# Nine weight pieces stored from another engine's queue, and one two-piece load split, in a recurrent-memory attention kernel

## The chip, the cores and the metric

The kernel runs on one core of a Trainium2 chip. The metric is the time of the whole program on the device in microseconds (us). The version before the change took a median of 2320.83 us in three runs (2319.13 to 2324.82).

## The reference, cut to what matters

Two independent branches see the same input `x` (2048 tokens of width 1024) and are mixed by a gate. Branch A is attention with 32 heads of 128 over segments of 32 tokens; eight memory rows, taken from the output of one segment, are put ahead of the next segment. So the 64 segments depend on each other. Branch B is a GeGLU feed-forward network of width 3584.

```python
for s in range(n_seg):                       # 64 segments, one after another
    h = concat([mem, x[:, 32*s:32*s+32]])    # 8 memory rows + 32 tokens
    q, k, v = h @ Wq, h @ Wk, h @ Wv         # each weight: 1024 x 32 x 128
    p = softmax(mask(q @ k.T * scale))
    o = (p @ v) @ Wo                         # Wo: 32 x 128 x 1024
    mem, out[s] = o[:, :8], o[:, 8:]
b = (gelu(x @ w_gate) * (x @ w_up)) @ w_down
return g * a + (1 - g) * b                   # g = sigmoid(sum(x * gate_w))
```

## The kernel before

**Segments.** One step of the kernel is one segment. A step's TensorE work has eight projections: `k`, `q`, `v` and `o`, each for two halves of 16 heads. `r` = 0 is the half that comes first in the step and `r` = 1 the other; which heads those are (`u`) alternates from step to step (`at_step`, L325). Each projection is cut into eight pieces of weights, 128 partitions x 2048 bf16 (512 KB). `walk` (L328) writes out the order of the pieces in a step: `HEAD` holds the first four pieces of `k`, two of `q`, the *last four pieces of the step before's second* `o`, and the rest of `k`, `q`, `v`; `BODY` holds the second halves of `k` and `q`, the first `o`, the second `v`, and the first four pieces of the second `o`. Everything else of a step (evacuations of PSUM, transposes, scores, softmax, attention, stores) is hung on a place of this walk: `on("o", 1, 0, f)` in `plan` (L903) emits `f` ahead of piece 0 of the second `o`. An engine executes its instructions in the order of emission.

**Fill.** Besides the step's own work TensorE projects 8 rows of each segment some steps ahead (`fill`, L844). The results are evacuated by ScalarE (`fill_evac`) into staging tiles, of which `0S` and `1S` lie over the tiles `hT` and `oRc`.

**Weights.** SBUF doesn't hold all pieces. A slot that two pieces share (`PAIRS`, L311: two of k, two of q, five of v, five of o) is loaded twice a step. When a piece has been used, `spent` (L442) emits the load of the slot's next one, on SP's queue. Pieces of neighbouring slots are loaded by one DMA: `GROUPS` (L372) tells how many. `spent` holds a used piece back until all of its group are used, and then `load_group` (L422, DMA on L429 from scratch or L433 from the inputs) loads them together, here Wo 0 and 1 (1 MB) and Wo 4, 5 and 6 (1.5 MB). Wo pieces that aren't all in scratch yet are loaded one by one (L385, L387). The first `o` uses pieces in pairs (0,4), (1,5), (2,6), (3,7) on L798 and frees 0 after the first pair, 1, 4, 5 after the second and 6 after the third. The second `o` (L815) uses 2, 3, 0, 1 in `BODY`, and 7, 4, 5, 6 in the next step's `HEAD`.

**Stores.** In the first steps each shared piece is written once from its slot to a scratch buffer of the group's layout (`keep`, L389, DMA on L391), so that later loads read long rows. Wo pieces are stored in steps 1 to 10 at `("k", 0, 4)`. The pieces of v, k and q (`STORE`, L901: v0 to v4, k0, k1, q0, q1, each for both halves) are stored in steps 3 to 20 at `("o", 1, 0)`, one a step: v in steps 3 to 12, k in 13 to 16, q in 17 to 20. All stores go through SP's queue and share one semaphore lane, so each waits for the landing of the store before. A load into a slot waits until the slot's store has landed.

**Behind the stores on SP.** At `("o", 1, 0)` SP also issues the load of `qkr` for the next step (L542) and the store of `oRc` to `o_scr` (L991). ScalarE's evacuation into `0S` or `1S` (L663) has to wait for that last store to land, TensorE transposes the tile on L680, and the next loads of k, q and v follow on SP.

The rest of the program (the output projection of eight rows of each segment, and the feed-forward network from L1074) isn't touched.

Of the kernel before, what the change touches and what calls it, by code (L numbers as in the profile page):

```python
# [30 lines left out]
class _Prog:  # L31
# [47 lines left out]
    def op(self, eng, fn, rd=(), wr=(), lane=None, after=()):  # L79
        o = _Op(eng, fn)  # L80
        if lane is not None:
            ln = self.lanes.get(lane)
            if ln is None:
                ln = self.lanes[lane] = [self.new_sem(f"{self.name}_{lane}"), 0, None]
            if ln[2] is not None:
                o.deps.append(ln[2])
            ln[1] += 16
            o.sem, o.val, o.inc, o.need = ln[0], ln[1], 16, True
            ln[2] = o
        for r in rd:  # L90
            self._touch(o, r, False, lane is not None)
        for r in wr:
            self._touch(o, r, True, lane is not None)
        o.deps.extend(after)
        if eng == "pool" and lane is None:
            if self.pool is not None:
                o.deps.append(self.pool)
            self.pool = o
        for d in o.deps:
            d.need = True  # L100
        o.idx = len(self.ops)
        self.ops.append(o)
        return o
# [107 lines left out]
def bass_gated_mix__memory_aug_recurrent_mem_tr__geglu_ffn__prompt_kernel(  # L211
# [16 lines left out]
    S, D = xf.shape  # L228
# [17 lines left out]
    with ExitStack() as es:  # L246
# [78 lines left out]
        def at_step(s, m, r, n):  # L325
            return (m, r ^ (s % 2), seq(m, r)[n])

        walk = []  # L328
        for s_ in range(NSEG):
            for m, r, lo, hi in HEAD + BODY:  # L330
                e = s_ - ((m, r, lo) == ("o", 1, 4))
# [20 lines left out]
        for _, e, m, r, n in walk:  # L352
            k = at_step(e, m, r, n)
# [3 lines left out]
        op = P.op  # L357
# [11 lines left out]
        def dst(t, k):  # L369
            return t[:, :].rearrange("p (h f) -> p h f", h=4) if k[0] == "o" else t[:, :]  # L370

        GROUPS = {("k", 0): 2, ("q", 0): 2, ("v", 0): 3, ("v", 3): 2, ("o", 0): 2, ("o", 4): 3}  # L372
        lead = {(m, i + x): (m, i) for (m, i), n in GROUPS.items() for x in range(n)}
        for (m, i), n in GROUPS.items():
            assert all(home[m, 0, i + x] == home[m, 0, i] + x for x in range(n))
        run_scr = {g: nc.dram_tensor(f"{g[0]}{g[1]}_scr", [2, 128, n, 2048], BF16) for g, n in GROUPS.items()}
        kept = set()

        def at_scr(k):
            g = lead[k[0], k[2]]  # L380
            return run_scr[g][k[1], :, k[2] - g[1], :]
# [4 lines left out]
            else:  # L386
                op("sp", lambda e: e.dma_start(dst(t, k), src(k)), wr=[t.r()], lane=lane)  # L387

        def keep(k):  # L389
            t = slots[home[k]]  # L390
            op("sp", lambda e: e.dma_start(at_scr(k), t[:, :]), rd=[t.r()], wr=[("D", "w", k)], lane="wo")  # L391
            kept.add(k)

        assert NSEG % 2 == 0
# [21 lines left out]
        def due(n):  # L416
            if done[n] < len(uses[n]) and uses[n][done[n]] != uses[n][done[n] - 1]:
                nk = uses[n][done[n]]
                return nk, nk in moved and done[n] == len(uses[n]) - 1
            return None, False  # L420
# [21 lines left out]
        def spent(k):  # L442
# [8 lines left out]
            q.append((n, *due(n)))  # L451
            if len(q) == GROUPS[g]:
                del held[g]
# [13 lines left out]
        for g in range(4):  # L467
            q = slice(32 * g, 32 * g + 32)
# [76 lines left out]
        def load_v(s, us=slice(0, 2), eng="pool"):  # L545
# [7 lines left out]
           wr=[gwb.r()], lane="gw")  # L553
# [3 lines left out]
        for n in range(8):  # L557
# [9 lines left out]
           rd=[memT.r()], wr=[hT0.r()])  # L567
# [122 lines left out]
        nm, sm = st8[:, 0, :], st8[:, 1, :]  # L690
# [210 lines left out]
        STORE = [(m, i) for m in "vkq" for i in PAIRS[m]]  # L901

        def plan(s):  # L903
            last = s == NSEG - 1
            ua, ub = s % 2, 1 - s % 2
# [6 lines left out]
            def on(m, r, n, *fs, s=s):  # L912
                at.setdefault((s, m, r, n), []).extend(fs)
# [19 lines left out]
            if not last and s == 0:  # L933
                on("k", 0, 4, lambda: load_h(s + 1))
            if 3 <= s < 3 + 2 * len(STORE):
                on("o", 1, 0, lambda: keep((STORE[(s - 3) // 2][0], ub, STORE[(s - 3) // 2][1])))
            if 1 <= s <= 2 * len(PAIRS["o"]):
                on("k", 0, 4, lambda: keep(("o", s % 2, PAIRS["o"][(s - 1) // 2])))
            on("q", 0, 4, lambda: evac(bank_of["k", 0], stage["k"], "act"))
# [49 lines left out]
            if not last:  # L989
                on("o", 1, 0, lambda: load_qk(s + 1, 0, "sp"))  # L990
            on("o", 1, 0, lambda: op("sp", lambda e: e.dma_start(o_scr[s], oRc[:, :, :].rearrange("p c x -> p (c x)")),  # L991
                                     rd=[oRc.r()], wr=[("D", "o", s)], lane="sto"))
# [13 lines left out]
            if two:  # L1006
# [4 lines left out]
                                     wr=[("D", "a", s)], lane="st"), **nx)  # L1011

        for s in range(NSEG):
            plan(s)
        for _, e, m, r, n in walk:
# [6 lines left out]
           wr=[("D", "a", NSEG - 1)], lane="st")  # L1022

        load_oR(NBK - 1)
        for b in range(NBK):
            rb = rbs[b % 2]
            for hf in range(2):
# [11 lines left out]
                for g in (2 * hf, 2 * hf + 1):  # L1039
                    op("act", lambda e, b=b, g=g, rb=rb: e.dma_start(a_scr[SB * b:SB * b + SB, g, NR:SEG, :], rb[0:RB, 256 * g:256 * g + 256]),  # L1040
                       rd=[rb.r(256 * g, 256 * g + 256)] + [("D", "a", t) for t in range(SB * b, SB * b + SB)], wr=[("D", "ar", b, g)],
                       lane=f"sr{g}")
# [32 lines left out]
        for fb in range(NFB):  # L1075
            HB, DN = ((0, 1, 2, 3), (4, 5, 6, 7)) if fb % 2 == 0 else ((4, 5, 6, 7), (0, 1, 2, 3))
            for j in range(NJ):
                c, cc = jch[j][0], jch[j][1] * 128
                bg, bu = HB[2 * (j % 2)], HB[2 * (j % 2) + 1]
                for bk, w in ((bg, wg[c]), (bu, wu[c])):  # L1080
# [8 lines left out]
                t = tp[j % 2]  # L1089
# [4 lines left out]
                   rd=[BK(bg), s1.r()], wr=[t.r()])  # L1094
# [3 lines left out]
                   rd=[BK(bu), t.r()], wr=[t.r()])  # L1098
                op("dve", lambda e, hg=hg, t=t, gt=gt: e.scalar_tensor_tensor(out=gt, in0=t[:, :], scalar=0.5, in1=hg,  # L1099
                                                                             op0=ALU.mult, op1=ALU.mult),  # L1100
                   rd=[BK(bg), t.r()], wr=[GT.r(j * FB, (j + 1) * FB)])
# [24 lines left out]
            for ps in range(NPS):  # L1126
                bank = DN if ps == 0 else HB
                tbs = [x for x in (2 * ps, 2 * ps + 1) if x < TB]
                for c in range(NWD):
                    w = wd[((fb * NPS + ps) * NWD + c) % 3]  # L1130
# [51 lines left out]
```

## Time and profile before

| | |
|---|---|
| median of three runs | 2320.83 us |
| the profiled execution | 2315.04 us, span 2313.2 us |
| TensorE clock granted over the span | 0.977 |
| PE, DVE, ACT, POOL busy | 2066.6, 1044.6, 541.8, 425.0 us |
| DMA | 647.46 MB, mean 280 GB/s |
| HBM read, written | 596.85 MB, 46.07 MB |
| chain that ended last | PE 59%, DMA 29%, DVE 5% |
| steps 3 to 20, from one issue of L991 to the next | 26.23 us on average (202.34 to 648.30 us, 17 steps) |
| steps 20 to 62 | 23.56 us on average (648.30 to 1637.78 us, 42 steps) |

PE is TensorE, PEld its weight loads, DVE is VectorE, ACT ScalarE, POOL GpSimd, SP SyncE; a `q` behind the name is the engine's instruction queue. `out<-in` are the program's names of tiles: `wall` holds the slots of Wo, `sl` those of k, q and v, `o_scr`, `v_scr`, `k_scr`, `q_scr` are scratch buffers in HBM. The profile gives the same label `o_scr` to the scratch of Wo's groups and to the buffer into which `oRc` is stored. PE and PEld often wait for the same thing, so their waits aren't added.

### The profile page before, as it was taken

How to read it: one execution, taken by the hardware profiler on the slowest of the kernel's cores; microseconds unless marked ns; L12 is line 12 of the kernel's file. 1: busy time of each engine (PE TensorE's matmuls, PEld its weight loads, DVE VectorE, ACT ScalarE, POOL GpSimd, SP SyncE). 2: the span in 40 equal slices, each digit the busy share in tenths (PEclk: the TensorE clock that was granted, in tenths of full speed). 3: DMA queues.
4: the chain of work that ended last, by engine and by line, in shares of the span. 5: the costliest groups of instructions: out<-in, count | busy, mean ns of one | idle time of the engine just before them, and what ended most of it. 6: DMA issues, size and time to landing. Idle time of an engine off the chain costs nothing.

```text
span 2313.2 us, 69748 instructions
## 1 busy us (share of the span) xinstructions
PE 2066.6 (89%) x31368; PEld 988.2 (43%) x31393; DVE 1044.6 (45%) x2697; ACT 541.8 (23%) x1111; POOL 425.0 (18%) x819
## 2 busy tenths in 40 slices
PE   3588888888899998999989989898899999999999
PEld 2243344434344444444444444443464444444444
DVE  3344344444444444545454544454316346163462
ACT  1122222222222222222222222222113123032130
POOL 4422212122222322222222222221100000000000
PEclk9699999999999999999999999999899999999999
DMA  9999999988998988899898999898964440803520
GB/s 372 354 306 337 340 328 357 342 311 319 327 341 333 354 335 339 333 343 347 328 344 335 345 334 351 331 358 330 336 210 152 144 157 10 288 21 121 174 88 19
DMA packets 198505, 647.46 MB, mean 280 GB/s; under 512 B 20760, under 2 KB 89624, under 8 KB 158784
## 3 DMA queue, kind: packets, MB, share of 16 engines
q1 hardware_dynamic: 174384, 606.02, 71.8%
q0 software_dynamic: 13888, 26.31, 3.4%
q10 hardware_dynamic: 9936, 10.69, 1.3%
q8 instruction: 247, 4.05, 0.7%
q14 instruction: 50, 0.41, 0.1%
HBM read 596.85 MB, written 46.07 MB: 278 GB/s over the span
## 4 chain that ended last, share of the span: by engine, by line
PE 59%; DMA 29%; DVE 5%; issue 2%; ACT 2%; POOL 1%; SPq 0%; ACTq 0%; POOLq 0%
PE pb L782 20%; PE pb L1083 15%; DMA wall<-o_scr 10%; PE pb L1137 5%; DMA o_scr<-oRc 4%; DMA qkr<-qk_scr 4%; PE pb L798 3%; PE pb L680 3%; DMA sl<-in_A_Wv_dram 3%; PE pb L815 3%; PE pb L1033 2%; PE pb L1118 2%; PE pb L852 2%; DMA xr_scr<-xr 1%; DMA wall<-in_A_Wo_dram 1%
## 5 line engine op out<-in xcount | busy, mean ns | idle before, releaser
L782 PE MATMUL pb<-sl,hT 128*32 128x512 bf16 x12288 | 774.7, 387 | 26.1 <-DMA sl<-in_A_Wv_dram 12.0
L782 PEld LDWEIGHTS pb<-sl,hT 128*32 128x32 bf16 x12288 | 312.9, 97 | 340.2 <-issue 28.6
L852 PE MATMUL pb<-sl,hR 128*32 128x512 bf16 x3072 | 219.1, 393 | 2.1 <-issue 1.5
L1083 PE MATMUL pb<-xT,wg 128*128 128x512 bf16 x896 | 211.7, 379 | 0.8
L1083 PE MATMUL pb<-xT,wu 128*128 128x512 bf16 x896 | 211.7, 379 | 0.0
L815 PE MATMUL pb<-wall,oT 128*32 128x256 bf16 x4056 | 157.0, 281 | 39.7 <-DMA wall<-o_scr 27.7
L663 ACT ACTIVATE kS<-pb 128x512 bf16<-128x512 f32 x127 | 75.8, 597 | 395.7 <-PE pb L782 373.2
L826 DVE COPY part<-pb 64x256 f32<-64x256 f32 x128 | 54.0, 422 | 252.5 <-PE pb L815 251.6
L765 POOL COPY oRc<-oT 128x128 bf16<-128x128 bf16 x128 | 96.5, 754 | 317.5 <-DVE oT L666 313.5
L798 PE MATMUL pb<-wall,oT 128*32 128x512 bf16 x2048 | 147.2, 385 | 5.8
L1137 PE MATMUL pb<-wd,GT 128*128 128x512 bf16 x657 | 144.8, 379 | 2.9 <-DMA wd<-in_B_w_down_dram 2.1
L815 PEld LDWEIGHTS pb<-wall,oT 128*32 128x32 bf16 x4056 | 98.0, 99 | 103.8 <-ACT oT L663 26.6
L1091 ACT ACTIVATE s<-pb 128x512 f32<-128x512 f32 x112 | 66.8, 596 | 312.2 <-PE pb L1083 312.2
L716 ACT ACTIVATE E<-pb 128x320 bf16<-128x320 f32 x128 | 56.0, 437 | 333.1 <-DVE pb L715 333.1
L1083 PEld LDWEIGHTS pb<-xT,wg 128*128 128x128 bf16 x896 | 87.2, 98 | 107.9 <-DVE GT L1099 3.7
L1092 DVE SCALAR_TENSOR_TENSOR tp<-s,pb 128x512 f32<-128x512 f32 x112 | 77.0, 687 | 124.7 <-ACT s L1091 124.5
L1083 PEld LDWEIGHTS pb<-xT,wu 128*128 128x128 bf16 x896 | 87.7, 98 | 105.7
L881 POOL COPY kT<-qkr 128x128 bf16<-128x128 bf16 x128 | 37.6, 294 | 499.9 <-DMA qkr<-qk_scr 259.9
L666 DVE COPY kT<-pb 128x512 bf16<-128x512 bf16 x128 | 54.4, 425 | 160.9 <-PE pb L680 160.9
L728 DVE STREAM_TRANSPOSE tAB<-pAB 128x128 bf16<-128x128 bf16 x512 | 114.1, 280 | 4.4
L666 DVE CAST oT<-pb 128x160 bf16<-128x160 f32 x256 | 76.5, 320 | 83.7 <-PE pb L748 83.7
L1096 DVE SCALAR_TENSOR_TENSOR tp<-tp,pb 128x512 f32<-128x512 f32 x112 | 77.1, 688 | 78.4 <-ACT tp L1095 78.4
(103 smaller groups left out, 2158.7 us busy)
## 6 DMA issues: line engine op xcount, KB each, us to landing
sl<-v_scr SPq DMA_DIRECT2D x55, 1536.0 KB, 10.1
wall<-o_scr SPq DMA_DIRECT2D x53, 1536.0 KB, 9.4
wall<-o_scr SPq DMA_DIRECT2D x59, 1024.0 KB, 5.5
sl<-v_scr SPq DMA_DIRECT2D x51, 1024.0 KB, 9.6
sl<-k_scr SPq DMA_DIRECT2D x47, 1024.0 KB, 5.5
sl<-q_scr SPq DMA_DIRECT2D x43, 1024.0 KB, 7.7
wd<-in_B_w_down_dram SPq DMA_DIRECT2D x42, 1024.0 KB, 5.5
sl<-in_A_Wq_dram SPq DMA_DIRECT2D x21, 1024.0 KB, 9.2
```

Of the source, the lines that this page charges most:

```text
L663: op("act", lambda e: e.activation(o, i, ACTF.Copy), rd=rd, wr=wr)
L666: op("dve", lambda e: e.tensor_copy(o, i), rd=rd, wr=wr, after=after)
L728: return [op("dve", lambda e, c=c: e.transpose(tAB[:, c + 32 * k:c + 32 * k + 4 * w].rearrange("p (j x) -> p j x", j=4)[:, :, 0:32], pAB[: ...
L765: op("pool", lambda e: e.tensor_copy(oRc[:, :, 16 * u:16 * u + 16].rearrange("p c x -> p x c"), oT[:, :, :, 32:40].rearrange("p g j c -> p ...
L782: ins = e.matmul(PB[bk][32 * g:32 * g + 32, :], lhsT=h[:, i, :], rhs=w[:, g * 512:(g + 1) * 512], start=(n == 0), stop=(n == 7))
L798: ins = e.matmul(PB[XO][32 * g:32 * g + 32, :], lhsT=oT[:, j, x, 0:32], rhs=wall[:, na:nb + 1:nb - na, c:c + 256], start=(n == 0 and hp == 0),
L815: ins = e.matmul(PB[XO][32 * g:32 * g + 32, 256 * b:256 * b + 256], lhsT=oT[:, j, x, 0:32], rhs=w[:, c:c + 256], start=False, stop=(n % 4 ...
L852: ins = e.matmul(PB[b][32 * g:32 * g + 32, :], lhsT=h[:, k[2], :], rhs=w[:, g * 512:(g + 1) * 512], start=(n == 0), stop=(n == 7))
L1083: ins = e.matmul(PB[bk][:, 0:FB], lhsT=w[:, kc, cc:cc + 128], rhs=xT[:, :, :, kc, :].rearrange("p t i c -> p (t i) c"), start=(kc == 0), s ...
L1092: op("dve", lambda e, hg=hg, t=t: e.scalar_tensor_tensor(out=t[:, :], in0=s1[:, :], scalar=1.0, in1=hg, op0=ALU.add, op1=ALU.mult), rd=[BK ...
L1096: op("dve", lambda e, hu=hu, t=t: e.scalar_tensor_tensor(out=t[:, :], in0=t[:, :], scalar=1.0, in1=hu, op0=ALU.add, op1=ALU.mult), rd=[BK( ...
L1137: ins = e.matmul(PB[bank[2 * k + hf]][:, :], lhsT=GT[:, j, tb * 128:(tb + 1) * 128], rhs=w[:, jj, hf * 512:(hf + 1) * 512], start=(j == 0) ...
```

## The change

`GROUPS` splits the group of Wo 0 and 1: each is loaded alone, by a DMA of 512 KB, as soon as it has been used. The group of Wo 4, 5 and 6 stays. `keep` gets the issuing engine as an argument; stores of v, k and q pieces go through ACT's queue, v at `("o", 1, 2)` and k and q at `("v", 1, 4)`, and have a semaphore lane of their own. Stores of Wo stay on SP at their place. The number of bytes moved is the same.

```diff
-        GROUPS = {("k", 0): 2, ("q", 0): 2, ("v", 0): 3, ("v", 3): 2, ("o", 0): 2, ("o", 4): 3}
+        GROUPS = {("k", 0): 2, ("q", 0): 2, ("v", 0): 3, ("v", 3): 2, ("o", 0): 1, ("o", 1): 1, ("o", 4): 3}
...
-        def keep(k):
+        def keep(k, eng="sp"):
             t = slots[home[k]]
-            op("sp", lambda e: e.dma_start(at_scr(k), t[:, :]), rd=[t.r()], wr=[("D", "w", k)], lane="wo")
+            op(eng, lambda e: e.dma_start(at_scr(k), t[:, :]), rd=[t.r()], wr=[("D", "w", k)], lane=f"keep{eng}")
             kept.add(k)
...
             if 3 <= s < 3 + 2 * len(STORE):
-                on("o", 1, 0, lambda: keep((STORE[(s - 3) // 2][0], ub, STORE[(s - 3) // 2][1])))
+                sm, si = STORE[(s - 3) // 2]
+                on(*(("o", 1, 2) if sm == "v" else ("v", 1, 4)), lambda: keep((sm, ub, si), "act"))
```

## The prediction

> **What bounds the kernel now.** I read the page first. In the lines of its parts 1, 2 and 4 PE is nearly always busy while the attention steps run, and so are the DMA engines:
>
> ```profile
> PE 2066.6 (89%) x31368; PEld 988.2 (43%) x31393; DVE 1044.6 (45%) x2697; ACT 541.8 (23%) x1111; POOL 425.0 (18%) x819
> DMA  9999999988998988899898999898964440803520
> PE 59%; DMA 29%; DVE 5%; issue 2%; ACT 2%; POOL 1%; SPq 0%; ACTq 0%; POOLq 0%
> ```
>
> So PE sets the pace, and what can be won is its waits for DMA. The steps with stores (3 to 20) take 26.23 us against 23.56 later: 2.67 us more, 48 us in 18 steps, part of it for slower loads from the inputs, the store's own bytes, and queueing.
>
> Next the table by stretches, for a step without a store (the L991 before it starts at 935.0). Columns: length, busy time of PE, PEld, DVE, ACT, POOL, granted clock, DMA share, GB/s:
>
> ```profile
> 950.00:952.50 2.50, 2.30 (x62) 1.18 (x65) 1.49 (x5) 0.99 (x3) 0.29 (x1) 1.00 0.82 330
> 952.50:954.50 2.00, 2.00 (x60) 1.02 (x53) 1.23 (x4) 0.44 (x1) 0.98 (x2) 1.00 0.39 95
> 954.50:961.00 6.50, 6.32 (x146) 3.18 (x142) 3.54 (x13) 1.69 (x4) 3.28 (x6) 1.00 0.99 409
> 961.00:963.00 2.00, 1.86 (x52) 1.13 (x44) 0.09 (x1) 0.03 (x1) 0.23 (x1) 1.00 0.59 142
> ```
>
> DMA isn't full: it runs at 409 GB/s while Wo is loaded, but falls to 95 for 2 us before that and to 142 after. The first hole lies between the end of v's loads and Wo's first load, issued at 952.59 by the timeline (lines of PE and SP):
>
> ```profile
> 950.92 0.62 PE L798 MATMUL pb<-wall,oT 128*32 128x512 bf16 x8
> 951.93 0.61 PE L798 MATMUL pb<-wall,oT 128*32 128x512 bf16 x8
> 952.59 1.35 SPq L429 DMA_DIRECT2D wall<-o_scr  x2
> ```
>
> The first L798 group frees Wo 0 at 951.54, the second frees Wo 1 at 952.54; the 1 MB load needs both. Data flows 1.9 us after the issue.
>
> Then the waits. For 199 to 672 us (steps with stores) those of SP's queue and of PE, then for 672 to 1676 us PE's (who, for whom, us in all, times, longest):
>
> ```profile
> SPq L143 <- DMA k_scr<-sl: 23.8, 4, 6.5
> SPq L143 <- DMA q_scr<-sl: 13.2, 4, 4.4
> SPq L143 <- DMA v_scr<-sl: 10.5, 5, 3.2
> ```
>
> ```profile
> PE pb L815 <- DMA wall<-o_scr: 11.4, 14, 1.7
> PE pb L680 <- ACT 1S L663: 9.6, 4, 3.3
> PE pb L680 <- ACT 0S L663: 7.3, 5, 1.9
> ```
>
> ```profile
> PE pb L815 <- DMA wall<-o_scr: 16.3, 22, 1.9
> ```
>
> SP stood still for 37 us until a k or q store had landed, before it could load those slots again. The chain shows why `0S` and `1S` are late in store steps: oRc's store (step 13) took 7.75 us, in a step without a store (32) 4.67.
>
> ```profile
> 463.23 7.75 DMA o_scr<-oRc
> 935.01 4.67 DMA o_scr<-oRc
> ```
>
> **The change, part by part.**
>
> *Split of Wo 0 and 1.* The pair is loaded as a group from step 5 on (59 DMAs of 1024 KB). Now Wo 0 goes 1.0 us earlier (951.54 against 952.54), Wo 1 as before; 0.5 MB at 409 GB/s is 1.28 us, so from then on the ring is full, and Wo 0, Wo 1 and the group 4 to 6 behind them land up to 1.0 us earlier where the hole is there, as in the table. Where v's loads run into Wo's, only Wo 0 lands sooner, by its half of the transfer, and PE can do its first eight L815 and a transpose (0.33 us) ahead of Wo 1. In 672 to 1676 PE waited 22 times for Wo, 0.74 us on average and 1.9 at most. Nearly all are under the 1.0 us; I take 12 of the 16.3 us away and leave 1 of it for the next wait (oRc's store is queued behind Wo and comes earlier too, so it isn't the one): **-11 us**, bounds 0 and -16. In steps 5 to 20 the queue is fuller (share 0.94 of the stretch against 0.90), so 4 of the 11.4 us: **-4**, bounds 0 and -11. The additional issue costs SP 0.32 us (L429) in a time in which SP waits for L798 anyway (80.5 us in 81 waits): nothing. Without that cover it would be 59 x 0.32 = 19 us.
>
> A rule of the Trainium skill speaks against it: "DMA: Bandwidth & Descriptors", under its measured bandwidths, advises batching to at least 1 MiB, with a fixed cost of about 2 us for each DMA. The rows that bear on it disagree for queued transfers: at 356 to 361 us four separate 512 KB pieces of Wo move at 415 GB/s, at 954.5 to 961 the groups at 409. By the rule the split alone would cost some 59 x 2 us, as an estimate; by the rows nothing. It stands as a rival.
>
> *k and q stores (8 steps).* On ACT they are issued once the exponential (L716) is done, at about 954.3 in the step above, 0.4 us behind the second Wo load; before, SP issued them at about the same point (458.32, 1 us after Wo) but behind 2.5 MB on the same ring. On a ring of its own a store shares the engines with the loads and should land at half to two thirds of the Wo train instead of behind it; by then neither slot is due. So the 37 us of SP's waits go. What that is worth to PE: k and q are needed only in BODY, 8 us later, and PE waits little for them. From the steps around 13 to 16 I take 1.0 us for each k store and 0.5 for each q store, **-6 us**. Bounds: -37/2 if half of SP's delay reached PE, and +8 x 1.28 = +10 if the store's bytes pushed Wo back each time. oRc's store comes behind the same bytes as before, so `0S` and `1S` win only the 1.0 us of the split.
>
> ACT pays an issue, 0.33 us on L522 (xq's stores), between L716 and the evacuation of vA, where it sits idle for 1.74 us. Queued behind it is that evacuation, for which PE's L740 waits; uncovered, 8 x 0.33 = 3 us. The instruction's own waits (the slot's load, already used by PE; the store one step earlier) are over by then.
>
> *v stores (10 steps).* On ACT they come behind the takes and the fill's evacuation: 958.2 in the step above, against L991 at 958.50. Before, SP issued them about 3 us ahead of L991 (199.37 against 202.34) behind Wo. The ACT queue's next work is `1S`, idle 4.79 us before it: the issue is free. oRc's store no longer has 0.5 MB ahead of it on its ring, but the store now interleaves with the end of Wo and with oRc. Gain at most 10 x 1.28 = -13; loss at most the same where Wo 4 to 6 is what PE waits for, plus SP's wait at the reload of v, 6.8 us behind L991 (965.26), if the store takes longer than that (before: 8.6 at least, most of it queueing). I take **0**, the middle, as in half of the steps `0S`/`1S` and in half Wo is waited for last.
>
> *Clock.* In the stretch 199 to 672 the granted clock was 0.97, in 672 to 1522 0.99, and it halves behind long waits: after PE's waits of 0.92 and 2.40 us (468.47 and 471.71) it is 0.50 from 471 to 477.5. Fewer such waits: **-2 us**, 0 to -10.
>
> Sum: -11 - 4 - 6 + 0 - 2 = -23 us. On the profiled execution, 2315.04 becomes 2292; it lies 5.8 us under the median, so on the median of the runs 2320.83 - 23 = **2298 us**.
>
> **Rivals.**
> *Only the split pays* (stores worth nothing): -11 - 4 + 2 = -13, 2308 us. For it: PE's waits for Wo are direct, SP's are not.
>
> *Hidden anyway*: PE meets the next wait, VectorE's fold (L836 behind L827) or `kT`'s copy on POOL behind qkr's load, and 4 or 5 us are left: 2316. For it: in many steps PE waits for nothing large and still takes 23.5 us.
>
> *Slower: the stores hold Wo back.* ACT's ring takes its turn at the engines, so a store that was last in line now goes between Wo's pieces: 1.28 us in each of 18 steps, +23, of which the split gives back 15: +8, 2329 us. It decides if the store's data starts before Wo's last is in, and Wo 4 to 6 is the last thing that PE waits for. For: 954.3 is ahead of the loads' end at 961. Against: PE waited only 14 times for Wo in that stretch, 0.8 us each, and oRc behind it decides in half of the steps.
> On this the Trainium skill ("DMA: Bandwidth & Descriptors", "Issuing engines are not separate DMA queues") says that all issuers' transfers interleave on the same 16 engines and only issue time is saved; the before trace has no large store on ACT's queue in these steps that could show it.
>
> *The split costs a transfer.* If the second DMA didn't follow at once but with the 1.9 us from issue to data, 59 x 1.9 less the gain, over +90 us: 2410. Only the skill's rule is for it; 415 against 409 GB/s is against.
>
> **How the numbers follow.** Chances: the forecast 0.50, only the split 0.17, hidden 0.12, stores hold Wo back 0.18, split costs 0.03. The forecast's own range is 2280 to 2308; with the hidden case and the +8 the range is 2278 to 2330. A measurement here can tell about 0.3% (7 us) from no change: faster 0.50 + 0.17 + a little = 0.68, same 0.12, slower 0.20.
>
> **What would show it.** Right: L429's Wo 0 load right behind the first L798 group; DMA over 300 GB/s where the table has 95; waits of L815 for Wo under 6 us after step 20; no SP wait on k's and q's stores; steps 13 to 20 about 1 us shorter. Wrong: Wo landing later in steps 3 to 20, L815 waits there over 20 us, ACT's vA or oT evacuations behind a DMA issue, or steps after 20 unchanged at 23.5 us.

## The result: 1.3% faster, and the profile after

The changed kernel took 2289.80 us (median of four runs, 2287.66 to 2293.32), the kernel before 2319.98 us beside it; the ratio is 0.9871, with a 95% interval of 0.9847 to 0.9896. A second measurement on another chip gave 0.9851 (0.9823 to 0.9880). So some 30 to 35 us are gone; 23 were forecast. The profiled execution took 2290.05 us, its span 2288.2 us, and the granted clock was 0.981 (before 0.977).

The page of the changed kernel, the lines that answer to those shown of before:

```profile
PE 2059.4 (90%) x31393; PEld 989.7 (43%) x31393; DVE 1044.2 (46%) x2697; ACT 541.9 (24%) x1111; POOL 423.5 (19%) x819
DMA  9999999989999999999999999998963530804520
PE 61%; DMA 27%; DVE 5%; issue 3%; ACT 2%; POOL 1%; ACTq 0%; SPq 0%; POOLq 0%
```

PE has the same work in a span that is 25 us shorter (and is busy 7 us less for it, 2059.4 against 2066.6 us), and DMA's share of the chain is down from 29 to 27%.

The table by stretches, at the same place of a step without a store as before (the stretches are set by the first L798 group, here at 912.32):

```profile
911.40:913.90 2.50, 2.30 (x63) 1.18 (x67) 1.49 (x5) 0.99 (x3) 0.29 (x1) 1.00 0.99 397
913.90:915.90 2.00, 2.00 (x60) 1.02 (x52) 1.23 (x4) 0.44 (x1) 0.97 (x2) 1.00 0.68 194
915.90:922.40 6.50, 5.50 (x120) 2.49 (x112) 3.78 (x13) 1.69 (x4) 1.78 (x3) 1.00 0.99 371
```

The hole ahead of Wo is half filled: 194 GB/s where before had 95. Both steps are near the low end of their kernel: over the steps between 700 and 1600 us the same 2 us (from 1.58 us after the first L798 group's start) carry 139 GB/s on average before, 272 after (DMA shares of 0.58 and 0.87). The timeline (lines of PE and SP) shows what fills it: the first of three loads now follows the first L798 group, 912.98 against a group that starts at 912.32, and no longer the second.

```profile
912.32 0.61 PE L798 MATMUL pb<-wall,oT 128*32 128x512 bf16 x8
912.98 2.05 SPq L429 DMA_DIRECT2D wall<-o_scr  x3
```

The waits, in the steps after the stores (660 to 1656 us), and in those with stores (195 to 660 us):

```profile
PE pb L815 <- DMA wall<-o_scr: 8.5, 16, 1.6
```

```profile
PE pb L815 <- DMA wall<-o_scr: 13.5, 16, 2.2
PE pb L815 <- DMA wall<-in_A_Wo_dram: 9.1, 8, 2.7
PE pb L680 <- ACT 1S L663: 5.9, 4, 3.2
PE pb L680 <- ACT 0S L663: 4.1, 5, 1.3
```

After step 20, PE's waits for Wo are half of what they were (16.3 us). In the steps with stores they have *grown*, from 13.3 us to 22.6 (both with the loads from the inputs), and the waits for `0S` and `1S` have shrunk, from 16.9 to 10.0. And SP still stands and waits for k's and q's stores to land (199 to 660 us; L143 is the line on which a queue's waits are written):

```profile
SPq L143 <- DMA k_scr<-sl: 20.9, 4, 7.7
SPq L143 <- DMA v_scr<-sl: 9.7, 6, 2.7
SPq L143 <- DMA q_scr<-sl: 7.5, 4, 2.3
```

So the first half of the change did in kind what was said of it, and the second half didn't.

### The profile page after: what moved, and what is told of

It is laid out like the page before. It is cut to its first block, busy times and chain, and to the rows that moved or that the text cites. A ratio compares the mean times of both kernels' runs of the same rounds, so it can differ in the third digit from the quotient of the medians.

```text
span 2288.2 us, 69892 instructions
## 1 busy us (share of the span) xinstructions
PE 2059.4 (90%) x31393; PEld 989.7 (43%) x31393; DVE 1044.2 (46%) x2697; ACT 541.9 (24%) x1111; POOL 423.5 (19%) x819
## 4 chain that ended last, share of the span: by engine, by line
PE 61%; DMA 27%; DVE 5%; issue 3%; ACT 2%; POOL 1%; ACTq 0%; SPq 0%; POOLq 0%
PE pb L782 21%; PE pb L1084 15%; DMA wall<-o_scr 8%; PE pb L1138 5%; DMA qkr<-qk_scr 4%; DMA o_scr<-oRc 4%; PE pb L798 4%; PE pb L680 3%; PE pb L815 3%; PE pb L852 3%; PE pb L1034 2%; DMA wall<-in_A_Wo_dram 2%; PE pb L1119 2%; DMA sl<-in_A_Wv_dram 2%; DMA xr_scr<-xr 1%
## 5 line engine op out<-in xcount | busy, mean ns | idle before, releaser
L782 PE MATMUL pb<-sl,hT 128*32 128x512 bf16 x12288 | 773.5, 387 | 20.9 <-DMA sl<-in_A_Wv_dram 9.1
L815 PE MATMUL pb<-wall,oT 128*32 128x256 bf16 x4056 | 152.7, 279 | 38.6 <-DMA wall<-o_scr 22.0
L798 PE MATMUL pb<-wall,oT 128*32 128x512 bf16 x2048 | 147.0, 384 | 6.0
L815 PEld LDWEIGHTS pb<-wall,oT 128*32 128x32 bf16 x4056 | 97.7, 98 | 98.5 <-ACT oT L663 25.9
```

The lines of the kernel that those rows point to most:

```text
L782: ins = e.matmul(PB[bk][32 * g:32 * g + 32, :], lhsT=h[:, i, :], rhs=w[:, g * 512:(g + 1) * 512], start=(n == 0), stop=(n == 7))
L798: ins = e.matmul(PB[XO][32 * g:32 * g + 32, :], lhsT=oT[:, j, x, 0:32], rhs=wall[:, na:nb + 1:nb - na, c:c + 256], start=(n == 0 and hp == 0),
L815: ins = e.matmul(PB[XO][32 * g:32 * g + 32, 256 * b:256 * b + 256], lhsT=oT[:, j, x, 0:32], rhs=w[:, c:c + 256], start=False, stop=(n % 4 ...
```

## The experiments

A profile is one execution, and its clock and waits vary; the verdicts rest on the ratios, and the profiles say where the time lies. "Clock" is the granted clock of the profiled execution. "3-12", "13-20" and "20-62" are the mean time of a step, from one issue of oRc's store to the next, from the timelines of SP: from that of step 3 to that of step 13, from that of step 13 to that of step 20, and from that of step 20 to that of step 62.

| kernel | ratio, 95% interval | clock | 3-12 | 13-20 | 20-62 |
|---|---|---|---|---|---|
| before | 1 | 0.977 | 26.09 | 26.44 | 23.56 |
| stores only | 0.9973, 0.9954 to 0.9992 | 0.975 | 26.78 | 25.44 | 24.08 |
| only v's stores | 0.9993, 0.9975 to 1.0010 | 0.974 | 26.46 | 26.01 | 24.02 |
| only k's, q's stores | 0.9982, 0.9960 to 1.0004 | 0.977 | 26.07 | 26.20 | 23.76 |
| two loads, held | 1.0102, 1.0079 to 1.0124 | 0.975 | 26.02 | 26.37 | 24.48 |
| two loads, held, own rows | 1.0023, 1.0001 to 1.0045 | 0.973 | 26.42 | 26.20 | 23.98 |
| split only | 0.9838, 0.9816 to 0.9860 | 0.979 | 25.69 | 25.17 | 23.55 |
| split only, again | 0.9859, 0.9827 to 0.9892 | 0.984 | 25.30 | 26.12 | 23.33 |
| changed kernel | 0.9871, 0.9847 to 0.9896 | 0.981 | 25.58 | 25.98 | 23.30 |
| changed kernel, again | 0.9851, 0.9823 to 0.9880 | 0.978 | 25.59 | 25.59 | 23.49 |
| split, v's stores on ACT | 0.9845, 0.9820 to 0.9869 | 0.980 | 25.80 | 25.78 | 23.36 |
| split, Wo 6 alone | 0.9888, 0.9862 to 0.9914 | 0.981 | 25.45 | 25.20 | 23.43 |
| all of Wo one by one | 0.9890, 0.9846 to 0.9935 | 0.979 | 25.42 | 26.13 | 23.40 |
| k's, q's stores in the hole | 0.9802, 0.9772 to 0.9833 | 0.983 | 25.21 | 24.46 | 23.23 |

### The two halves of the change by themselves

The split alone:

```diff
-        GROUPS = {..., ("o", 0): 2, ("o", 4): 3}
+        GROUPS = {..., ("o", 0): 1, ("o", 1): 1, ("o", 4): 3}
```

> The groups of the changed kernel (Wo 0 and 1 loaded one by one), all stores on SP as before. Theory A (the split pays in every step from 5 on, because it fills the hole in the DMA work ahead of Wo; the stores pay the rest in steps 3 to 20): ratio 0.992 to 0.994, some -15 us, with steps 20 to 62 as short as in the changed kernel (23.3 us) and steps 3 to 20 only about 0.2 us a step shorter than before. Theory B (the split carries everything, the place of the stores is worth nothing): ratio 0.986 to 0.989. Theory C (the stores carry most of it): 0.996 or more.

The stores alone keep the old `GROUPS` and take the new `keep` and its places:

```diff
...
-                on("o", 1, 0, lambda: keep((STORE[(s - 3) // 2][0], ub, STORE[(s - 3) // 2][1])))
+                sm, si = STORE[(s - 3) // 2]
+                on(*(("o", 1, 2) if sm == "v" else ("v", 1, 4)), lambda: keep((sm, ub, si), "act"))
```

> The stores of v, k and q as in the changed kernel (ACT's queue, new places), Wo 0 and 1 as one group as before. Theory A: ratio 0.994 to 0.997, some -10 us, all of it in steps 3 to 20, and PE's waits for Wo after step 20 as before (16 us). Theory B: 0.998 to 1.001. Theory C: 0.990 or less.

The split alone measured 0.9838, all of the change's gain and as the point value a little more; the stores alone 0.9973. The two don't add: 0.9838 x 0.9973 would be 0.981, and the changed kernel is at 0.987 and 0.985. That is the rival theory B, but with the split below the 0.986 to 0.989 that B gave it, and with stores that are worth some 6 us where the group of Wo 0 and 1 is still there.

PE's waits, split only (672 to 1640 us) and then stores only (the same stretch):

```profile
PE pb L815 <- DMA wall<-o_scr: 12.2, 17, 1.8
```

```profile
PE pb L815 <- DMA wall<-o_scr: 27.5, 26, 2.7
```

In the five profiles with the early load held back or absent (before, the three with stores alone, and the held loads with rows of their own, which come below; the first held version, at 1.0102, had 35.1) these waits are 16.3, 27.5, 23.0, 19.4 and 22.4 us, 21.7 on average; in the five with the split and Wo 4 to 6 in one group at the change's places of the stores or before's (12.2, 10.4, 8.5, 12.2, 12.0) 11.1. The profile that the prediction was made from had the least of all without the split.

### Which stores

v's stores alone, and k's and q's alone, each with the old `GROUPS`:

```diff
+                if sm == "v":
+                    on("o", 1, 2, lambda: keep((sm, ub, si), "act"))
+                else:
+                    on("o", 1, 0, lambda: keep((sm, ub, si)))
```

> Wo 0 and 1 as one group; only the ten stores of v go to ACT's queue at their new place, k and q stay on SP. If oRc's store gains by no longer having the v store ahead of it on SP's ring: ratio 0.996 to 0.998, -5 to -9 us, and the waits for 0S and 1S in steps 3 to 12 fall by half. If the interleaving with Wo takes as much as that gives: 0.999 to 1.001.

```diff
+                if sm == "v":
+                    on("o", 1, 0, lambda: keep((sm, ub, si)))
+                else:
+                    on("v", 1, 4, lambda: keep((sm, ub, si), "act"))
```

> Wo 0 and 1 as one group; only the eight stores of k and q go to ACT's queue at their new place, v stays on SP. In the changed kernel SP still waited 20.9 us for k's and 7.5 us for q's stores (before 23.8 and 13.2), since the store on ACT's ring landed only with the end of Wo 4 to 6. If that wait is what matters: ratio 0.999 to 1.001, within 2 us. If ACT's ring pays by relieving oRc's store (no longer behind the store on SP's ring): 0.996 to 0.998.

Neither can be told from before (0.9993 and 0.9982), and SP's wait for k's stores is 23.6 us with k and q on ACT, against 23.8. Worked out from the traces' issues and landings, as medians over steps 13 to 20 counted from the end of the first L798 group: on SP (before) a k or q store is issued at 2.0 and lands at 14.0 us, the last Wo at 12.1 and oRc at 14.7; on ACT, issued at 2.5, it lands at 13.6, Wo at 13.5 and oRc at 14.0. The same bytes pass in about the same time; Wo is later by 1.4 us, the store sooner by 0.4 and oRc by 0.7.

### Does the early start pay, or the smaller transfer?

Here Wo 0 and 1 are two DMAs, but both wait for the second L798 group:

```diff
+                if g == ("o", 0) and not any(mv for _, _, mv in q) and all(nk in kept for _, nk, _ in q):
+                    for x in q:
+                        reload(*x)
...
```

Each of these two loads is also given a wait for the L798 group that frees Wo 1.

> Wo 0 and 1 are loaded by two DMAs of 512 KB as in the changed kernel, but both wait until the second L798 group has freed Wo 1, so the first no longer starts 1.0 us earlier; stores on SP as before. Theory H (the gain comes from the earlier start, which fills the hole ahead of Wo): most of the gain is gone, ratio 0.994 to 1.000. Theory G (the gain comes from the finer landing: PE can start on Wo 0 alone, without an earlier start): ratio near that of the split alone, 0.984 to 0.988. Half of each: 0.990 to 0.993.

That was 1.0102, slower than before, outside of every theory's range. The scratch there still had the pair's layout, so a piece was read in rows of 4 KB at steps of 8 KB. A second version gives each piece a scratch of its own, as the changed kernel does, and differs from the split alone only in the start of Wo 0:

```diff
+        GROUPS = {..., ("o", 0): 1, ("o", 1): 1, ("o", 4): 3}
-                    for x in {1: (0,), 3: (1, 4, 5), 5: (2, 6), 7: (3, 7)}[n]:
+                    for x in {1: (), 3: (0, 1, 4, 5), 5: (2, 6), 7: (3, 7)}[n]:
...
+            after = used[0] if m == "o" and n == 1 else []     # the L798 group that frees Wo 1
```

> As the held pair (two DMAs of 512 KB, both only when Wo 1 is free, stores on SP), but with the scratch of Wo 0 and 1 laid out piece by piece, as in the changed kernel, so that each DMA reads one contiguous 512 KB and not 4 KB rows at 8 KB steps. If the loss of the held pair (1.0102) comes from the strided rows: 0.998 to 1.001. If it comes from two smaller DMAs in place of one: 1.006 to 1.012. Either way an early start is what pays if this one isn't faster than before.

1.0023: two transfers in place of one win nothing and cost 0 to 10 us. The same two transfers with the first one started 1.0 us earlier give 0.9859 on the same chip. So the start is what pays, 1.6% by these two. The timeline of the held version (SP) has all three loads behind the second L798 group, at 957.30; the table by stretches has the hole at its place in that step, 1.58 us behind the first group at 956.29:

```profile
957.96 1.58 SPq L432 DMA_DIRECT2D wall<-o_scr  x3
```

```profile
957.87:959.87 2.00, 2.00 (x60) 1.21 (x60) 1.15 (x4) 0.44 (x1) 0.98 (x2) 1.00 0.57 164
```

Its L432 and L801 are L429 and L798 of the others. Over the steps between 700 and 1600 us these 2 us carry 160 GB/s on average in the held version and 269 in the split alone: held, the hole is open again. Worked out as medians over steps 24 to 59, from the end of the first L798 group: before, Wo's pair lands at 6.1 and its group of three at 11.1 us; with the split alone Wo 0 at 4.7, Wo 1 at 6.3, the three at 11.0; held, 4.8, 6.9 and 11.5. Two pieces in place of one pair bring Wo 0 to PE 1.3 us sooner even when it is held, but Wo 1 and the three 0.8 and 0.4 us later. The early start changes Wo 0 by only 0.1 us; it takes back that delay, 0.6 us of Wo 1 and 0.5 us of the three.

PE's waits say the same. Worked out from the traces for 672 to 1640 us, each wait of L815 put down to the load whose landing ended it:

| ended by | before | held, own rows | split only | split only, again |
|---|---|---|---|---|
| the pair, or Wo 0 | 6.7 | 0.7 | 0 | 0 |
| Wo 1 alone | | 7.7 | 3.2 | 3.6 |
| Wo 4 to 6 | 9.6 | 14.1 | 9.0 | 6.8 |

Held, the wait for the pair has only moved to Wo 1, and the one for the three has grown; started early, the first is under half of that and the second under two thirds. Over all profiles of the table above with the pair loaded as one (four) and with the early start at the change's or the old places of the stores (five), the first two rows together are 10.9 and 2.5 us on average, the last row 10.7 and 8.5.

### The changed kernel beside its variants

The changed kernel once more, the split with only v's stores on ACT, and the split with Wo 6 loaded alone (`("o", 4): 2, ("o", 6): 1`, stores on SP), all on one chip:

> The changed kernel once more, beside the others on the same chip. The split alone measured 0.9838 (0.9816 to 0.986), the changed kernel 0.9871 (0.9847 to 0.9896) on other chips. If the stores on ACT cost what they win once the split is there: 0.983 to 0.985; if they hold Wo back and so cost 5 to 8 us: 0.986 to 0.988; if they add their 0.9973 alone to the split: 0.981.

> The split, with v's stores on ACT's queue and k's and q's on SP as before. By the two profiles steps 13 to 20 (k, q) took 206.1 us in the changed kernel and 200.8 us with all stores on SP, steps 3 to 12 (v) 255.8 and 256.9. If the k and q stores on ACT are what costs: 3 to 6 us faster than the changed kernel beside it, ratio 0.982 to 0.984. If that difference of two profiles was chance: equal to it within 2 us.

> All stores on SP; Wo 0 and 1 one by one, and Wo 4 and 5 as a pair as soon as they are free (second L798 group), Wo 6 alone behind the third. The pair's load starts up to 0.6 us sooner than the group of three did, and Wo 4 can be used before Wo 6 is in. If an earlier start of the same bytes pays whenever the ring has room: 0.979 to 0.982, some 5 us better than the split alone. If the ring is already full by then, with Wo 0 and 1 in it: 0.983 to 0.985, no difference.

0.9851, 0.9845 and 0.9888. The first two can't be told apart from each other, nor from the split alone on its two chips (0.9838, 0.9859): beside the split the change's places of the stores are worth nothing measurable. Wo 6 alone, meant to let Wo 4 and 5 start sooner, doesn't help and is if anything slower. By its profile PE's waits for Wo are 8.6 us in 672 to 1640; what it loses for that isn't settled.

### Why the stores land late, and a better place

All of Wo's shared pieces one by one, stores as in the changed kernel:

```diff
+        GROUPS = {..., ("o", 0): 1, ("o", 1): 1, ("o", 4): 1, ("o", 5): 1, ("o", 6): 1}
```

> The changed kernel (stores on ACT) with Wo 4, 5 and 6 loaded one by one too, so that Wo's packets on SP's ring are 4 KB, as the store's on ACT's ring, and not 12 KB. Theory P (the two rings take turns by packets, so the store got a quarter of the engines beside 12 KB packets and landed with the end of Wo): k's and q's stores now land 2 to 4 us sooner than the 13.1 us of the changed kernel, at 9 to 11. Theory F (the store is late for another reason): they still land within 0.7 us of the last Wo. The time: 0.985 to 0.992, since smaller loads of Wo cost about what they win.

The k and q stores land at 11.5 us (median, counted as above), the last Wo at 13.4; in the changed kernel 13.1 and 13.3. So beside Wo's small packets the store leaves the train 1.9 us ahead of its end, where it came with the end of it before. That is the direction of theory P, and too much for F, but less than the 2 to 4 us that P gave. SP's wait for k's stores is 16.3 us (20.9 and 16.8 in the changed kernel's two profiles), and the time is no better, 0.9890.

The packets in the two traces show why the store is late. In steps 13 to 20 its first packet moves 3.6 to 4.8 us after its issue in both kernels. From then on it shares the engines with Wo. In step 13, in 455 to 458 us, while the store runs, the queues (packets, MB, share of the 16 engines) are these, first in the changed kernel and then with single pieces; q1 is SP's and q10, on which the store's 128 packets of 4 KB run, is ACT's:

```profile
q1 hardware_dynamic: 76, 0.86, 78.6%
q10 hardware_dynamic: 60, 0.25, 20.6%
```

```profile
q1 hardware_dynamic: 191, 0.68, 63.8%
q10 hardware_dynamic: 112, 0.43, 35.5%
```

Both move 1.13 MB in these 3 us. Beside Wo's packets of 12 KB the store has 22% of the bytes, beside those of 4 KB 38%. Turns packet by packet would give 25 and 50% (4 of 16 KB, 4 of 8 KB): the direction is measured, the exact rule isn't, and what holds the store's first packet for 4 us stays open.

The last kernel moves k's and q's stores to the start of the step's first `o`, so that their bytes come into the hole:

```diff
-                on(*(("o", 1, 2) if sm == "v" else ("v", 1, 4)), lambda: keep((sm, ub, si), "act"))
+                on(*(("o", 1, 2) if sm == "v" else ("o", 0, 0)), lambda: keep((sm, ub, si), "act"))
```

> The changed kernel with k's and q's stores moved once more, on ACT's queue to the place (o, 1, 0 of the first half: the start of the step's first o), so that their 1.28 us of transfer lies in what is left of the hole ahead of Wo instead of among Wo's loads; v as in the changed kernel. If the bytes there are free: Wo lands 1 us sooner in steps 13 to 20 than with the place of the changed kernel (13.2 us after Wo 0 is free in the four profiles with k and q on ACT, 11.6 to 12.4 with them on SP), SP's wait for k's store is gone, and the ratio is 0.980 to 0.983. If Wo 0 now waits behind them, as the hole is already taken by the split: no better than the split alone, 0.983 to 0.987.

0.9802, 2278.14 us (median of six runs): faster than the kernel before and, by 0.9802 against 0.9859 on the same chip, than the split alone by about 13 us; the intervals (up to 0.9833, from 0.9827) just touch. Steps 13 to 20 take 24.46 us, where no other kernel is under 25.1: 1.5 and 1.1 us less than in the changed kernel's two profiles, 10 to 12 us in eight steps. For the first of them, the table by stretches of before and of this kernel, the 2 us behind the second L798 group:

```profile
457.30:459.30 2.00, 2.00 (x60) 1.02 (x48) 1.23 (x4) 0.44 (x1) 0.98 (x2) 1.00 0.52 123
```

```profile
446.00:448.00 2.00, 2.00 (x52) 1.02 (x40) 1.28 (x3) 0.44 (x1) 0.98 (x2) 1.00 0.99 383
```

The hole is full. That does two things. First, SP's queue (timelines of before, of the changed kernel, and of this one, step 13; L992 is L991 of before): k's load stands behind k's store. It is issued 6.93, 8.05 and 3.83 us after oRc's store, and in this kernel SP has no wait for k's and q's stores left.

```profile
463.23 0.32 SPq L991 DMA_DIRECT2D o_scr<-oRc  x1
470.16 0.38 SPq L433 DMA_DIRECT2D sl<-in_A_Wk_dram  x1
```

```profile
455.28 0.32 SPq L992 DMA_DIRECT2D o_scr<-oRc  x1
463.33 0.38 SPq L433 DMA_DIRECT2D sl<-in_A_Wk_dram  x1
```

```profile
452.01 0.32 SPq L992 DMA_DIRECT2D o_scr<-oRc  x1
455.84 0.38 SPq L433 DMA_DIRECT2D sl<-in_A_Wk_dram  x1
```

Second, Wo's train ends sooner: the last Wo lands at 12.1 us and oRc at 12.7 (counted as above), against 13.3 and 13.9 in the changed kernel. PE's waits tell which of the two pays. From step 13's store of oRc to step 21's, in the changed kernel (455.3 to 661.4 us) and then in this one (452.0 to 646.4):

```profile
PE pb L815 <- DMA wall<-o_scr: 12.0, 12, 2.2
```

```profile
PE pb L815 <- DMA wall<-o_scr: 1.9, 3, 0.9
```

The changed kernel's second profile had 9.2. For pieces of k and q PE waited 0 and 0.6 us there, and not at all here. So beside the changed kernel it is Wo's earlier landing that PE gains from, and no gain shows from the end of SP's wait. Beside the split alone it is less clear: its two profiles have 1.5 and 5.1 us of waits for Wo in these steps, and 6.8 and 3.1 for pieces of q.

The split alone, again, ran beside it:

> The split with all stores on SP, once more, beside the others. Measured 0.9838 (0.9816 to 0.986) on another chip; the changed kernel 0.9871 and 0.9851. If the stores' place is worth nothing beside the split: 0.983 to 0.988.

0.9859, in the range of the first measurement: the stores' place in the changed kernel adds nothing to it.

## Why the prediction was right, and where its steps failed

**The signs.** Of the five signs of being right only the first came in full: Wo 0's load follows the first L798 group. DMA in the old hole is at 194 GB/s in the step shown and 272 on average, not over 300; L815's waits for Wo after step 20 are 8.5 and 12.2 us in the changed kernel's two profiles, not under 6; SP's waits for k's and q's stores stay; steps 13 to 20 are 0.5 and 0.9 us shorter, where about 1 was said. Of the signs of being wrong, Wo did land later in steps 13 to 20 (13.3 and 13.0 us against 12.1), and L815's waits in the steps with stores were over 20 us in one profile (22.6) and not in the other (12.6). The steps after 20 were hardly shorter than in the one profile of before (23.30 and 23.49 us against 23.56), which was the quickest there of all kernels without the early start (23.76 to 24.48 in the others). The time came out inside the stated range all the same, for the reasons that follow.

**The hole and the split: right in kind, too small.** The hole is half filled. The 11 us taken from PE's waits for Wo after step 20 are what the profiles show, but between other ends: 21.7 to 11.1 us on average, where the prediction read 16.3 and left 5. Little of it was hidden: in the same stretch PE's waits for VectorE rose by 2.5 us (34.4 to 36.9 on average). Two terms of the sum were mis-sized. The first is the clock: -2 us for the whole change. Over the span it was 0.977, 0.975, 0.974, 0.977 and 0.973 without the early start (as above, 0.9752 on average) and 0.979, 0.984, 0.981, 0.978 and 0.980 with it (0.9804): 0.0052 of 2300 us is 12 us, as an estimate, and PE's busy time for the same work agrees, 2071.5 us on average in the first five profiles and 2060.1 in the others, 11 us less. The second is steps 5 to 20, taken at -4: with all stores on SP, PE's waits for Wo in 199 to 660 us (both sources of Wo) were 13.3 and 12.4 us without the early start and 4.8 and 8.4 with it, 6 us less, and the steps 3 to 12 became 0.4 to 1.1 us shorter. With -11, -12 and -6 one comes to -29 us of the 33 to 38 of the split alone (0.9859 and 0.9838 of 2324); the rest isn't put down to a term. Both were sized from one execution, and at 2315.04 us it was the shortest of its chip's four runs (to 2324.82), with the fewest waits for Wo of the five. The text set the 5.8 us to the median aside as an offset; that they were part of what could be won is likely, not shown.

**"Land up to 1.0 us earlier": failed.** Only Wo 0 did (4.7 us against the pair's 6.1); Wo 1 was 0.2 us later and the three 0.1 us sooner. The prediction let two transfers of 512 KB take the time of one of 1 MB; held back, the second landed 0.8 us and the three 0.4 us later, and the kernel lost 0.2% (0.0 to 0.45%). The early start paid for that as well. So what PE gained is mostly that its first eight matmuls wait for Wo 0 alone and that Wo 1 is there, nearly as soon as the pair was, when they are done.

**The price of smaller transfers.** The held version measures it for this kernel: 1.0023, some 5 us for 59 additional DMAs, 0.09 us each. (59, as a slot that two pieces share is loaded once a step, not twice as the description of the kernel says: the half that ends a step begins the next.) The prediction weighed the advice of the Trainium skill ("DMA: Bandwidth & Descriptors", under its measured bandwidths) to batch to 1 MiB. That the held version isn't faster agrees with that advice. The fixed cost of about 2 us for each DMA that the Trainium skill gives ("DMA: Bandwidth & Descriptors", "Anatomy of one DMA", for DMAs issued by GpSimd) would be 118 us for 59, as an estimate. The 5 us measured don't agree with it, for loads from SP that queue behind others.

**k and q stores: wrong.** "Should land at half to two thirds of the Wo train" failed: the store landed with its end, 13.1 us against 13.3 for the last Wo, as its data began to move 4 us after the issue and then had a fifth of the engines. SP's 37 us of waits became 28. The -6 us weren't there: alone the k and q stores measured 0.9982 (0.9960 to 1.0004). The term was also put on a wait that hardly reached PE: before, in steps 13 to 20, PE waited 2.6 us for pieces of k and q from the inputs, against SP's 37. The last kernel, in which SP's wait is gone, gained 1.1 to 1.5 us a step there, but in PE's waits for Wo.

**v stores: 0 forecast**, 0.9993 (0.9975 to 1.0010) measured.

**The rivals.** "Only the split pays" was the right account of the mechanism, at 0.17, with too small a split. "The stores hold Wo back" was right in its mechanism too: with stores on ACT's queue PE's waits for Wo in the steps with stores were 28.6, 19.1 and 21.8 us without the split and 22.6, 12.6 and 11.3 with it, with all stores on SP 13.3 and 12.4 without the early start and 4.8 and 8.4 with it. It didn't decide, since `0S` and `1S` gained about as much: PE's waits for them were 9.6, 10.0 and 6.3 us with all stores on ACT, 16.9, 19.7, 13.2 and 16.1 with all on SP. The forecast's -23 us came out near the result in part by luck: -6 us for stores that gained nothing made up for part of a split with its clock that was put at -17 and measured -33 to -38.

## What to carry to other kernels

Look for the stretch in which the DMA engines idle although every queue has work to come, and ask what the next transfer waits for: here a 1 MB load waited for its second half to be free, and splitting it so that the first half starts 1.0 us sooner was worth 1.4 to 1.6%. Moving a transfer to another queue doesn't take its bytes from beside the others; putting it into the idle stretch does. And size a change from several executions, or at least ask whether the profiled one was a good one.

## What the runs showed of the hardware that I had not expected

A 512 KB store on ACT's ring, issued beside 2.5 MB of loads on SP's, took until the loads' end (k's and q's stores alone on ACT: issued at 2.5, landed at 13.6 us, the last load at 13.5). Its first packet moved some 4 us after the issue. Beside loads in packets of 12 KB it then had 22% of the bytes, beside packets of 4 KB 38%, and landed 1.6 us sooner (11.5 against 13.1).

Reading a piece in rows of 4 KB at steps of 8 KB instead of from a contiguous 512 KB cost 0.8% (1.0102 against 1.0023), 18 us for 59 pairs of loads, 0.3 us a pair. And the granted clock went with the waits: it was 0.9752 on average without the early start and 0.9804 with it, and PE's busy time for the same work was 11 us shorter, about a third of the split's gain.
